# A merged group of score products, and a newly planned order of all instructions, in a causal attention that feeds a gated feed-forward block

## The chip, the cores and the metric

The kernel runs on one core of one Trainium2 chip. The metric is the device time of one execution in microseconds (us), lower is better. The core has a matrix engine (PE, with its weight loads as PEld), a vector engine (DVE), a scalar engine (ACT), a general engine (POOL) and a sequencer that issues every load and store here (SP). Each engine runs its own list of instructions in a fixed order; between engines there are only semaphores.

## The reference

```python
def _attn_ref(q, k, v):                      # 4 x 12 x 448 x 64, float32
    scores = (1 / sqrt(64)) * q @ k.T        # per batch and head, 448 x 448
    scores = where(above the diagonal, -1e9, scores)
    attn = exp(scores - max(scores))
    attn = attn / (sum(attn) + 1e-09)
    return attn @ v
x = attention output, heads side by side     # 1792 x 768
a, b = x @ w1, x @ w2                        # w1, w2: 768 x 1024
h = a * b @ w3                               # w3: 1024 x 1024
return h @ w_out                             # w_out: 1024 x 768
```

There is nothing between `w3` and `w_out`, so the kernel multiplies these two once (the "w34" product) and applies the result.

## The kernel before

**Stages.** (1) w34: blocks of w3 (index `m`, 128 rows, loaded in two halves) and of w_out (index `g`) are loaded and decoded (`decode`: two readings by ACT, a shift on DVE, an add on DVE or POOL). Each half block of w3 is turned on PE (L768, four transposes into the one bank of the pool `tr`), copied out (L774 on ACT or L775 on DVE), and multiplied with the blocks of w_out in float32 (L780). The first three blocks `m` are kept open together, in six banks. (2) Attention: 24 pairs of heads, six to a batch element. A pair loads q and k, turns them (L492 on PE for the first 12 pairs, by DMA for the rest), makes scores, the running maximum (L592, DVE) and exponential (L596, ACT), normalises and splits into two float16 halves (L621 to L628), turns these by DMA, and multiplies with v (L648, L653). (3) For each batch element the gates `x @ w1` and `x @ w2` (L904 to L906) and (4) the projection (L964 to L966), in float16 with three terms.

**Shapes of the array.** Most products use PE as one array of 128 x 128. The scores of two heads run side by side on two arrays of 64 rows (`mode="row"`), those of the last 64 queries on four arrays of 64 x 64 (`mode="quad"`), the products with v on two of 64 columns (`mode="col"`). The first 12 pairs make scores in float32, the others in float16.

**Score groups.** `scores` (L565) makes one entry of the plan per group of score units: for a pair the groups (2, 5), (1, 4), (6,) and (0, 3). Units 0 to 2 are the three chunks of 128 queries of one head (128, 256 and 384 keys wide), 3 to 5 those of the other, unit 6 the last 64 queries of both. Each unit has a bank of its own of the pool `sc`.

**Order.** Nothing is scheduled by the compiler. `Program.add` gathers entries with a due time, a cost for each engine that may run them, and their dependences. `Program.order` then plays the plan through on modelled engines: at each step the engine that is free first takes the ready entry with the earliest due time. That sets the order on every engine, which engine does a thing that several could do, and the banks. Due times come from `PLAN`, a table of numbers. `hold` adds a dependence that keeps the loads of an early pair behind the load of a chosen block of w_out. An SP entry waits in SP's list: a load or a DMA transpose that cannot go yet holds up all behind it.

Of the kernel before, what the change touches and what calls it, by code (L numbers as in the profile page):

```python
# [14 lines left out]
F16 = mybir.dt.float16  # L15
# [11 lines left out]
PLAN = dict(nc=10, wstep=3.6064, soft=-6.8718, w0=50.8305, w34=0.7706, ab=1.9504, out=0.6632, gap=-1.6322, lat=44.2335, begin=-91.0074, wlead=70.5419, urgent=-469.9817, flex=370.3401, sc=-41.0893, vo=-494.4237, av=-194.2706, x=-353.7633, qlead=-514.025, rlead=417.269, v0=250.3178, v1=137.6978, gram=2, nf=3, h0=0, hv=1, ns=7, wo0=372.2276, wo1=301.1492, wom=91.9573, w3a=767.9653, w3l=46.2422, wd=-104.1576, wh=-132.8946, wl=1.1959, fin=-10.7242, ev=483.517, po=[7.835, -22.3194, -46.2642, -45.7187, -46.1544, -168.5123, 44.732, 118.2718, -2.1469, -154.505, -36.8352, 4.8443, 45.9944, -62.3407, -59.3789, -141.4965, -13.9926, -146.366, -84.3586, -180.0751, 32.2385, 37.7583, 62.9194, 45.468], wo=[94.042, -8.263, -88.9315, -217.7217, 115.6771, 99.8526, 211.7957, -24.8481], w3=[-158.8005, -50.8167, -61.9442, -32.663, -51.9857, -143.9432, 16.037, 208.3012], tw=[-214.4914, 58.2404, 21.4694, -22.4979, -112.6908, -172.2348, -114.743, -134.9378, -53.1451, -19.9257, -4.9187, -20.2346, -61.9799, -199.5703, -107.2525, -134.2498], slack=0.1918, pflex=136.6935, fq=2, hlead=80.6809, stick=24.2514, wfrom=6)  # L27
# [10 lines left out]
WINDOW, PHASE = 3.413, 1.65  # L38

# [11 lines left out]
class Program:  # L51
# [3 lines left out]
    def __init__(self):  # L55
        self.ops, self.writer, self.readers, self.modes = [], {}, {}, {}
        self.port, self.lock = set(), set()
        self.banks, self.leased, self.first = {}, [], {}
# [5 lines left out]
    def add(self, due, how, reads=(), writes=(), stage=None, mode=None, port=False, lock=False):  # L64
# [18 lines left out]
        if mode:  # L83
            self.modes[i] = mode
        if port:
            self.port.add(i)
# [11 lines left out]
    def order(self):  # L98
# [8 lines left out]
        free = {e: 0.0 for e in (PE, ACT, DVE, POOL, SP)}  # L107
        soon = {e: [] for e in free}
        avail = {e: {} for e in free}
        ran = [None] * n  # L110
        dma_free, last_mode, lock_end, port_end = 0.0, None, 0.0, 0.0
# [28 lines left out]
        while len(result) < n:  # L140
# [41 lines left out]
            if e == SP:  # L182
                move, turn = cost
                dma_free = max(dma_free, t + (1.275 if turn else 1.1)) + move
                free[e] = max(t + 0.65, dma_free - 0.93) if turn else t + 0.475
                end = dma_free + 0.91
            else:
# [9 lines left out]
                if e == PE and cost:  # L197
                    mode = self.modes.get(i)
                    if mode != last_mode:
                        cost += SWITCH  # L200
                        last_mode = mode
                    end = matmul(t, cost)
# [40 lines left out]
def tile_causal_attention_moe(ctx: ExitStack, tc: tile.TileContext, q, k, v, w1, w2, w3, wo, out):  # L243
# [196 lines left out]
    def dma(dst, src, due, reads, writes, size, turn=False, rate=330e3):  # L440
        kw = {"transpose": True} if turn else {}
        prog.add(due, (SP, (size / (181e3 if turn else rate), turn),
# [15 lines left out]
    def take_v(b, half, due):  # L458
# [7 lines left out]
        for c in range(4):  # L466
            rows = min(P, S - c * P)
            dma(t[0:rows, c], v[b, heads, c * P : c * P + rows].rearrange("h p d -> p h d"), due - 6, (), [vk[c]],
                NP * rows * D * 4, rate=181e3)
# [11 lines left out]
    def turned_whole(p, b, hs, T, qk, qkk, qt, qtk):  # L481

        for i, src in ((1, k), (0, q)):
            dma(qk[0:QP, i], src[b, hs].rearrange("h (p r) d -> p r h d", r=4),
                T - PLAN["qlead"], (), [qkk + (i,)], 2 * S * D * 4, rate=181e3)
# [15 lines left out]
    def halved(p, b, hs, T, qk, qkk, qt, qtk):  # L501
# [4 lines left out]
        for i, src in ((1, k), (0, q)):  # L506
            raw_k = [qkk + (i, n) for n in range(3)]
            for h in range(2):
                dma(qk[:, i, 0:3, h], src[b, hs.start + h, 0 : 3 * P].rearrange("(c p) d -> p c d", p=P), T - PLAN["qlead"],
                    [], [raw_k[h]], 3 * P * D * 4, rate=181e3)  # L510
            dma(qk[0:D, i, 3], src[b, hs, 3 * P : S].rearrange("h p d -> p h d"), T - PLAN["qlead"],
                [], [raw_k[2]], 2 * D * D * 4, rate=181e3)
# [23 lines left out]
    def pair(p):  # L536
# [28 lines left out]
        def scores(us, due):  # L565
            i, c, w, lo = place(us[0])
            n = min(P, S - c * P)
            banks = [prog.lease("sc") for _ in us]
            m = mask_t if i == 2 else mask[:, (2 - c) * P :]

            def products(qs, ks, start, stop):
                for j in range(2):
                    rows = slice(j * D, (j + 1) * D)
                    ps = banks[j if i < 2 else 0][0]
                    nc.tensor.matmul(ps[rows if i == 2 else slice(0, P), :w], qs[rows, c * P : c * P + n], ks[rows, 0:w],  # L575
                                     start=start, stop=stop)

            def both():
                if not halves:
                    products(qt[:, 0], qt[:, 1], True, True)  # L580
                    return
                q16 = qt.rearrange("p i f -> p (i f)").bitcast(F16).rearrange("p (i t f) -> p i t f", i=2, t=2)
                for m_, (a, b_) in enumerate(((0, 0), (0, 1), (1, 0))):
                    products(q16[:, 0, a], q16[:, 1, b_], m_ == 0, m_ == 2)

            outs = [heads[place(u)[0]] for u in us]
            prog.add(due, (PE, (3 if halves else 4) * t_mm(w) + 0.02, both), [qtk + (1,), qtk + (0,)],
                     [key for _, key in banks] + [tk + (c,) for _, tk in outs] + ([tk for _, tk in outs] if p < 2 else []),
                     mode="quad" if i == 2 else "row")
            for u, (ps, key), (t32, tk) in zip(us, banks, outs):  # L590
                o = t32[:, lo : lo + w]
                prog.add(due + 0.4, (DVE, t_dve(w) + 0.07, lambda o=o, ps=ps, u=u: nc.vector.tensor_tensor_reduce(  # L592
                    out=o, in0=ps[:, :w], in1=m, scale=iv, scalar=-NEG,
# [471 lines left out]
```

## Time and profile before

| | |
|---|---|
| three runs | 554.55, 555.80, 556.99 us, median 555.8 |
| profiled execution | 555.84 us, its span 554.0 us |
| PE busy | 537.5 us (97%), 3872 instructions |
| DVE, ACT, POOL busy | 384.4, 323.9, 156.1 us (69%, 58%, 28%) |
| chain that ended last | PE 82%, DVE 9%, ACT 3%, DMA 3% |
| bytes moved by DMA | 84.60 MB |

The span runs from the first to the last instruction; 1.84 us of the execution's own time lie outside of it. The chain follows the work back from the last instruction, at each step to what released it or to the instruction before it on its engine. PE's records begin when an instruction starts to stream, and their ends overlap the next one's start; distances are therefore read from start to start.

### The profile page before, as it was taken

What the parts mean: (1) busy time and instruction counts of PE and PEld (TensorE: products, weight loads), DVE (VectorE), ACT (ScalarE), POOL (GpSimd) and SP (SyncE); (2) the same over time, 40 slices, a digit from 0 to 9 for tenths busy, and PEclk for the clock granted to TensorE, in tenths of its full rate; (3) what the DMA queues carried; (4) which work ended last, traced back from release to release, by engine and by line L of the source; (5) the groups of instructions that cost most, each with busy time, mean ns of one, the idle gap of its engine ahead of it and who ended that gap; (6) DMA issues with size and microseconds to landing.
All of it is one profiled execution on the core that took longest, in us unless ns stands there. A gap on an engine that the chain in (4) does not pass through costs nothing.

```text
span 554.0 us, 10756 instructions
## 1 busy us (share of the span) xinstructions
PE 537.5 (97%) x3872; PEld 300.5 (54%) x3872; DVE 384.4 (69%) x1057; ACT 323.9 (58%) x774; POOL 156.1 (28%) x118
## 2 busy tenths in 40 slices
PE   2999999999999999999999999999999999999996
PEld 1565565555554555555445555655555555555564
DVE  5536999998999899984998768398986760322100
ACT  6757888798698978654664646265762551111111
POOL 4000465554566424430334203231421110000000
PEclk9999999999999999999999999999999999999999
DMA  8998599989989648998777958979899235000011
GB/s 324 289 298 233 118 217 206 229 215 240 184 216 239 153 97 151 180 178 167 107 155 142 166 128 167 185 164 159 142 142 143 61 84 115 0 2 1 14 58 43
DMA packets 224950, 84.60 MB, mean 153 GB/s; under 512 B 205952, under 2 KB 221824, under 8 KB 224896
## 3 DMA queue, kind: packets, MB, share of 16 engines
q1 hardware_dynamic: 224896, 83.91, 72.1%
q8 instruction: 30, 0.49, 0.4%
q14 instruction: 24, 0.20, 0.1%
HBM read 43.78 MB, written 5.51 MB: 89 GB/s over the span
## 4 chain that ended last, share of the span: by engine, by line
PE 82%; DVE 9%; ACT 3%; DMA 3%; issue 1%; POOL 1%; POOLq 0%; ACTq 0%
PE sc L575 8%; PE mm L780 8%; PE mm L904 7%; PE mm L905 7%; PE mm L906 7%; PE mm L964 5%; PE mm L966 4%; PE mm L965 4%; PE tr L904 4%; PE av L653 4%; PE tr L905 4%; PE tr L906 4%; PE sc L780 2%; PE tr L964 2%; PE tr L966 2%; PE tr L965 2%
## 5 line engine op out<-in xcount | busy, mean ns | idle before, releaser
L906 PE MATMUL mm<-xt,w 128*128 128x448 f16 x258 | 90.9, 352 | 1.3 <-DVE w L727 1.3
L904 PE MATMUL mm<-xt,w 128*128 128x448 f16 x258 | 91.1, 353 | 0.0
L905 PE MATMUL mm<-xt,w 128*128 128x448 f16 x258 | 90.9, 352 | 0.0
L596 ACT ACTIVATE p<-p,mx 128x384 f32<-128x384 f32 (+2 forms) x144 | 71.5, 497 | 28.7 <-DVE mx L592 28.6
L780 PE MATMUL mm<-wof,w3t 128*128 128x384 f32 x192 | 71.4, 505 | 2.5 <-POOL wof L688 2.5
L628 DVE SCALAR_TENSOR_TENSOR ph<-p,rc,ph 128x384 f16<-128x384 f32 (+2 forms) x144 | 68.6, 528 | 1.4 <-ACT ph L623 0.9
L625 POOL TENSOR_SCALAR ph<-p,rc 128x128 f16<-128x128 f32 (+2 forms) x40 | 43.1, 1086 | 69.8 <-DVE rc L606 39.5
L575 PE MATMUL sc<-qkt 64*128 64x384 f16 (+7 forms) x480 | 58.9, 356 | 0.2 <-DMA qkt<-da 0.2
L906 PEld LDWEIGHTS <-w 128*128 128x128 f16 x384 | 37.5, 98 | 37.1 <-DVE w L727 2.2
L904 PEld LDWEIGHTS <-w 128*128 128x128 f16 x384 | 37.5, 98 | 36.0 <-issue 3.5
L905 PEld LDWEIGHTS <-w 128*128 128x128 f16 x384 | 37.5, 98 | 29.7 <-issue 0.2
L964 PE MATMUL mm<-w34h,arena 128*128 128x384 f16 x152 | 49.7, 327 | 0.0
L966 PE MATMUL mm<-w34h,arena 128*128 128x384 f16 x152 | 49.5, 326 | 0.0
L965 PE MATMUL mm<-w34l,arena 128*128 128x384 f16 x152 | 49.5, 326 | 0.0
L780 PEld LDWEIGHTS mm<-wof,w3t 128*128 128x128 f32 x192 | 34.2, 193 | 24.3 <-issue 4.1
L904 PE MATMUL tr<-xt,w 128*128 128x448 f16 x126 | 44.5, 353 | 0.0
L905 PE MATMUL tr<-xt,w 128*128 128x448 f16 x126 | 44.4, 352 | 0.0
L906 PE MATMUL tr<-xt,w 128*128 128x448 f16 x126 | 44.4, 352 | 0.0
L592 DVE CUSTOM_DVE_ANT_0 p<-sc,mask,qiv 128x384 f32<-128x384 f32 (+2 forms) x72 | 31.4, 478 | 18.0 <-PE sc L575 17.8
L930 ACT CAST arena<-g 128x448 f16<-128x448 f32 x22 | 12.4, 563 | 49.2 <-DVE g L925 49.2
L623 ACT ACTIVATE ph<-p,rc 128x384 f16<-128x384 f32 (+2 forms) x64 | 29.1, 504 | 9.5 <-issue 5.7
L685 DVE TENSOR_SCALAR da<-da 128x768 int32<-128x768 int32 (+1 forms) x38 | 24.2, 639 | 14.9 <-ACT da L681 14.7
(182 smaller groups left out, 1028.8 us busy)
## 6 DMA issues: line engine op xcount, KB each, us to landing
arena<-in_moe_w_dram SPq DMA_DIRECT2D x11, 768.0 KB, 5.7
vr<-in_v_dram SPq DMA_DIRECT2D x24, 192.0 KB, 3.9
out_dram<-osb SPq DMA_DIRECT2D x24, 192.0 KB, 2.2
arena<-in_moe_w_dram SPq DMA_DIRECT2D x8, 512.0 KB, 5.1
xt<-in_moe_w_dram SPq DMA_DIRECT2D x5, 768.0 KB, 8.0
qkr<-in_k_dram SPq DMA_DIRECT2D x12, 224.0 KB, 6.3
qkr<-in_q_dram SPq DMA_DIRECT2D x12, 224.0 KB, 6.9
arena<-in_moe_w_out_dram SPq DMA_DIRECT2D x3, 768.0 KB, 9.3
```

The lines of the kernel that those rows point to most:

```text
L575: nc.tensor.matmul(ps[rows if i == 2 else slice(0, P), :w], qs[rows, c * P : c * P + n], ks[rows, 0:w], start=start, stop=stop)
L592: prog.add(due + 0.4, (DVE, t_dve(w) + 0.07, lambda o=o, ps=ps, u=u: nc.vector.tensor_tensor_reduce(out=o, in0=ps[:, :w], in1=m, scale=iv, ...
L596: prog.add(due + 0.9, (ACT, t_act(w, pointers=1, acc=True), lambda o=o, u=u: nc.scalar.activation(out=o, in_=o, func=AF.Exp, scale=-1.0, b ...
L625: (POOL, 1.1 * (t_pool(w) + 0.35e-3 * w + 0.16), lambda src=src, r=r, h=h: nc.gpsimd.tensor_scalar(out=h, in0=src, scalar1=r, scalar2=None ...
L628: prog.add(due + 0.4, (DVE, t_dve(w) + 0.06, lambda src=src, r=r, h=h, l=l: nc.vector.scalar_tensor_tensor(out=l, in0=src, scalar=r, in1=h ...
L780: prog.add(due, (PE, 4 * t_mm(NH), lambda: nc.tensor.matmul(ps[:, :NH], w3t[slot(m)][:, g], wof[:, g, ns], start=g == 0, stop=g == KF - 1) ...
L904: nc.tensor.matmul(ps[:, :S], w[:, 0, d], xh, start=d == 0, stop=False)
L905: nc.tensor.matmul(ps[:, :S], w[:, 0, d], xl, start=False, stop=False)
L906: nc.tensor.matmul(ps[:, :S], w[:, 1, d], xh, start=False, stop=d == KD - 1)
L964: nc.tensor.matmul(t, gh[:, fc, cs], w34h[:, fc, ns], start=fc == 0, stop=False)
L965: nc.tensor.matmul(t, gh[:, fc, cs], w34l[:, fc, ns], start=False, stop=False)
L966: nc.tensor.matmul(t, gl[:, fc, cs], w34h[:, fc, ns], start=False, stop=fc == KF - 1)
```

## The change

The plan's table has new numbers throughout, and the planner's model of loads is new: a begin time for each engine, a rate and a count of descriptors for each kind of load, and a limit (`RING`) past which SP is held back. The model only decides the order. Two parts change what is built: `scores` now takes several groups for one entry, and the groups (1, 4) and (0, 3) form one, whose 128 columns stand behind the 256 in the same bank; and the group (6,) may also take the bank of the pool `tr`. With `h0=-1` and `hv=0` the first pair's loads, and the first half of v, are no longer held behind a block of w_out.

```diff
-PLAN = dict(nc=10, wstep=3.6064, ..., gram=2, nf=3, h0=0, hv=1, ns=7, ...)
+PLAN = dict(nc=10, wstep=10.6096, ..., gram=2, nf=3, h0=-1, hv=0, ns=7, ..., join=0)
...
+BEGIN = {PE: 1.3, ACT: 2.1, DVE: 0.85, POOL: 1.3, SP: 0.5}
+RING = 2150
...
             if e == SP:
-                move, turn = cost
-                dma_free = max(dma_free, t + (1.275 if turn else 1.1)) + move
-                free[e] = max(t + 0.65, dma_free - 0.93) if turn else t + 0.475
+                move, turn, count = cost
+                begun = max(dma_free, t + (1.07 if turn else 1.22))
+                dma_free = begun + move
                 end = dma_free + 0.91
+                if turn:
+                    free[e] = max(t + 0.65, dma_free - 0.6 - 0.5 * move)
+                else:
+                    free[e] = t + (0.6 if count > 800 else 0.43)
...
-    def dma(dst, src, due, reads, writes, size, turn=False, rate=330e3):
+    def dma(dst, src, due, reads, writes, size, turn=False, rate=430e3, count=128):
...
-        def scores(us, due):
-            i, c, w, lo = place(us[0])
-            banks = [prog.lease("sc") for _ in us]
+        def scores(groups, due):
+            blocks = []
+            for us in groups:
+                i, c, w, lo = place(us[0])
+                if c == 0:
+                    shared, at = blocks[-1][1], blocks[-1][2] + blocks[-1][4][2]
+                else:
+                    shared, at = [prog.lease("sc") if i < 2 else prog.lease("sc", "tr") for _ in us], 0
+                blocks.append((us, shared, at, mask_t if i == 2 else mask[:, (2 - c) * P :], (i, c, w, lo)))
...
-        for n, us in enumerate(((2, 5), (1, 4), (6,), (0, 3))):
-            scores(us, T + PLAN["sc"] + 0.6 * n)
+        for n, groups in enumerate(([[(2, 5)], [(1, 4), (0, 3)], [(6,)]], [[(2, 5), (6,)], [(1, 4), (0, 3)]])[PLAN["join"]]):
+            scores(groups, T + PLAN["sc"] + 0.6 * n)
```

Line numbers move: L575 becomes L602, L780 becomes L814, L768 becomes L802, L443 becomes L463, L681 and L683 become L714 and L716, L774 becomes L808.

**PE, scores of the first pair, before.** In the w34 stage; `qkt` holds turned q and k, rows of L575 are scores, L780 are w34 products, L768 and L492 turns.

```order
L575 MATMUL sc_69<-qkt_84 128x384
L575 MATMUL sc_66<-qkt_84 128x384
L407 LDWEIGHTS ones
L407 MATMUL sc_67<-w34m_126,ones 128x1
L780 MATMUL sc_68<-wof,w3t_124 128x384
L780 MATMUL mm_64<-wof,w3t_122 128x384 x2
L575 MATMUL sc_69<-qkt_84 128x256
L575 MATMUL sc_66<-qkt_84 128x256
L780 MATMUL mm_64<-wof,w3t_122 128x384
L768 MATMUL tr_70<-ident,arena 128x128 x4
L780 MATMUL mm_64<-wof,w3t_122 128x384
L575 MATMUL sc_67<-qkt_84 128x128
```

The same engine in the change, where the first pair's scores stand ahead of nearly all products of the stage:

```order
L602 MATMUL sc_66<-qkt_84 128x384
L602 MATMUL sc_67<-qkt_84 128x384
L602 MATMUL tr_70<-qkt_84 64x448 x2
L814 MATMUL mm_64<-wof,w3t_122 128x384
L814 MATMUL mm_65<-wof,w3t_122 128x384
L802 MATMUL tr_70<-ident,arena 128x128 x4
L602 MATMUL sc_66<-qkt_84 128x256
L602 MATMUL sc_67<-qkt_84 128x256
L602 MATMUL sc_66<-qkt_84 128x128
L602 MATMUL sc_67<-qkt_84 128x128
```

The 256- and 128-wide scores follow each other in one bank, and the tail (64x448) stands directly behind the 384-wide ones, in the bank `tr`.

**SP, the first loads, before.** `in_moe_w_dram` is w3 here, `in_moe_w_out_dram` w_out; the name on the left is the buffer that the raw words land in.

```order
L443 DMA arena<-in_moe_w_dram 128x1024 x2
L443 DMA xt_101<-in_moe_w_out_dram 128x1536
L443 DMA w34h<-in_moe_w_dram 128x1024
L443 DMA w34l<-in_moe_w_dram 128x1024
L443 DMA w34h<-in_moe_w_out_dram 128x1536
L443 DMA w34l<-in_moe_w_dram 128x1024
L443 DMA arena<-in_moe_w_dram 128x1024
L443 DMA arena<-in_moe_w_out_dram 128x1536
L443 DMA qkr_82<-in_k_dram 112x8x64
L443 DMA qkr_82<-in_q_dram 112x8x64
```

And in the change:

```order
L463 DMA w34l<-in_moe_w_dram 128x1024
L463 DMA arena<-in_moe_w_dram 128x1024 x2
L463 DMA xt_101<-in_moe_w_out_dram 128x1536
L463 DMA w34h<-in_moe_w_out_dram 128x1536
L463 DMA w34h<-in_moe_w_dram 128x1024
L463 DMA w34l<-in_moe_w_dram 128x1024
L463 DMA qkr_82<-in_k_dram 112x8x64
L463 DMA qkr_82<-in_q_dram 112x8x64
L463 DMA arena<-in_moe_w_dram 128x1024
L463 DMA arena<-in_moe_w_out_dram 128x1536
```

A half of the third w3 block (512 KB) now stands ahead of the two halves of the first; k and q of the first pair moved ahead of the third block's other half.

**ACT in the same stretch, before.** L681 and L683 are the two readings of a raw buffer, L774 copies turned w3 out of the bank `tr`.

```order
L683 ACTIVATE w34h<-w34h 128x768
L681 ACTIVATE da_107<-w34l 128x512
L774 COPY w3t_123<-tr_70 128x512
L683 ACTIVATE w34l<-w34l 128x512
L681 ACTIVATE da_108<-arena 128x512
L774 COPY w3t_123<-tr_70 128x512
```

In the change:

```order
L714 ACTIVATE p_88<-w34l 128x512
L716 ACTIVATE w34l<-w34l 128x512
L714 ACTIVATE da_108<-arena 128x512
L716 ACTIVATE arena<-arena 128x512
L808 COPY w3t_123<-tr_70 128x512
L714 ACTIVATE da_106<-arena 128x768
```

The first copy into `w3t_123` stands behind both readings of the third block's second half (`da_108`, `arena`); before it stood ahead of them.

## Rows read from the trace of the kernel before

**Rows 1.** PE's waits: line, for whom, us in total, times, longest.

```profile
PE tr L768 <- DVE arena L688: 6.7, 1, 6.7
...
PE mm L906 <- DVE w L727: 1.3, 2, 1.0
```

**Rows 2.** Stages: stretch, its length, then busy us of PE, PEld, DVE, ACT, POOL.

```profile
20.00:50.00 30.00, 29.94 (x116) 17.62 (x114) 11.84 (x20) 18.55 (x30) 1.28 (x1) 1.00 1.16 286
50.00:140.00 90.00, 90.00 (x569) 52.09 (x569) 84.01 (x231) 76.48 (x188) 45.47 (x29) 1.00 0.93 200
140.00:250.00 110.00, 108.53 (x849) 60.32 (x848) 104.77 (x285) 85.69 (x196) 52.50 (x33) 1.00 0.86 174
250.00:480.00 230.00, 229.78 (x1921) 126.13 (x1920) 163.85 (x488) 117.34 (x322) 51.23 (x42) 1.00 0.72 133
```

**Rows 3.** Timeline of PE, float32 part: start us, duration us, line, count.

```profile
52.91 0.70 PE L575 MATMUL sc<-qkt 64*128 64x256 f32 x4
53.54 0.91 PE L780 MATMUL mm<-wof,w3t 128*128 128x384 f32 x2
...
62.09 0.92 PE L575 MATMUL sc<-qkt 64*128 64x384 f32 x4
62.94 0.91 PE L780 MATMUL mm<-wof,w3t 128*128 128x384 f32 x2
63.69 0.60 PE L768 MATMUL tr<-ident,arena 128*128 128x128 f32 x4
...
72.92 1.35 PE L575 MATMUL sc<-qkt 64*128 64x256 f32 x8
74.20 0.91 PE L780 MATMUL mm<-wof,w3t 128*128 128x384 f32 x2
```

**Rows 4.** Timeline of PE, float16 products of the gates ahead of scores.

```profile
176.63 0.35 PE L905 MATMUL mm<-xt,w 128*128 128x448 f16 x1
176.82 0.35 PE L906 MATMUL mm<-xt,w 128*128 128x448 f16 x1
177.11 1.35 PE L575 MATMUL sc<-qkt 64*128 64x384 f32 x8
```

**Rows 5.** Chain that ended last, first 22 us: start us, duration us, what.

```profile
4.58 0.66 ACT da L681
...
6.67 1.10 PE tr L768 x4
...
12.01 2.93 PE mm L780 x4
...
15.83 0.59 ACT w3t L774
...
18.42 1.29 PE mm L780 x4
...
21.39 0.44 PE tr L768 x4
21.83 0.38 PE sc L492 x4
```

**Rows 6.** Landing times of the first two loads, issued at 0.73 and 1.19.

```profile
DMA to landing us min/median/max: 3.8/4.2/4.6
```

**Rows 7.** Loads issued from 7.7 to 9.2, and their times to landing.

```profile
L443 SPq DMA_DIRECT2D arena<-in_moe_w_out_dram x1: 328/328/328, 7.8 to 7.8; - x1
...
L443 SPq DMA_DIRECT2D qkr<-in_q_dram x1: 3105/3105/3105, 9.0 to 9.0; - x1
...
DMA to landing us min/median/max: 9.4/10.2/10.5
```

**Rows 8.** Groups by line and form on DVE and POOL: busy us, mean ns.

```profile
L621 DVE TENSOR_SCALAR ph<-p,rc 128x384 f16<-128x384 f32 x14 | 8.4, 608 | 0.1
...
L688 DVE CUSTOM_DVE_ANT_0 wof<-arena,da 128x1536 uint16<-128x1536 uint16 x3 | 2.9, 960 | 0.8 <-ACT arena L683 0.8
...
L688 POOL TENSOR_TENSOR wof<-da,xt 128x768 int32<-128x768 int32 x1 | 1.8, 1847 | 6.9 <-ACT xt L683 6.9
```

More of the change, by code (lines that the diff above doesn't have):

```diff
@@ L62, in lease, with add @@
         return l, l
[L64 removed]
+    def add(self, due, how, reads=(), writes=(), stage=None, mode=None, leave=None, port=False, lock=False):
         how = how if isinstance(how, list) else [how]
@@ L84, in add @@
             self.modes[i] = mode
+            self.leave[i] = leave or mode
         if port:
@@ L106, in order @@
         ready_at, done = [0.0] * n, [False] * n
-        free = {e: 0.0 for e in (PE, ACT, DVE, POOL, SP)}
+        free = dict(BEGIN)
         soon = {e: [] for e in free}
@@ L200, in order @@
                         cost += SWITCH
-                        last_mode = mode
+                    last_mode = self.leave.get(i)
                     end = matmul(t, cost)
@@ L574, in products @@
                     ps = banks[j if i < 2 else 0][0]
-                    nc.tensor.matmul(ps[rows if i == 2 else slice(0, P), :w], qs[rows, c * P : c * P + n], ks[rows, 0:w],
+                    nc.tensor.matmul(ps[rows if i == 2 else slice(0, P), at : at + w], qs[rows, c * P : c * P + n], ks[rows, 0:w],
                                      start=start, stop=stop)
             def both():
-                if not halves:
-                    products(qt[:, 0], qt[:, 1], True, True)
-                    return
@@ L582, in both @@
[L582 to L593, printed above, removed]
-                    op0=ALU.add, op1=ALU.min, accum_out=mx[:, u : u + 1])),
-                    [key, ivk, "mask_t" if i == 2 else "mask"], [mk + (u,), tk + (c,)] + ([tk] if p < 2 else []))
-                prog.add(due + 0.9, (ACT, t_act(w, pointers=1, acc=True), lambda o=o, u=u: nc.scalar.activation(
-                    out=o, in_=o, func=AF.Exp, scale=-1.0, bias=mx[:, u : u + 1], accum_out=sm[:, u : u + 1])),
-                    [mk + (u,)], [tk + (c,), smk + (u,)])
+                for block in blocks:
+                    if not halves:
+                        products(block, qt[:, 0], qt[:, 1], True, True)
+                        continue
+                    q16 = qt.rearrange("p i f -> p (i f)").bitcast(F16).rearrange("p (i t f) -> p i t f", i=2, t=2)
+                    for m_, (a, b_) in enumerate(((0, 0), (0, 1), (1, 0))):
+                        products(block, q16[:, 0, a], q16[:, 1, b_], m_ == 0, m_ == 2)
@@ new lines, in scores @@
+            keys = {id(l): l for b_ in blocks for _, l in b_[1]}
+            outs = [(heads[place(u)[0]][1], b_[4][1]) for b_ in blocks for u in b_[0]]
+            mode = ["quad" if b_[4][0] == 2 else "row" for b_ in blocks]
+            cost = sum((3 if halves else 4) * t_mm(b_[4][2]) + 0.02 for b_ in blocks) + SWITCH * (mode[0] != mode[-1])
+            prog.add(due, (PE, cost, both), [qtk + (1,), qtk + (0,)],
+                     list(keys.values()) + [tk + (c,) for tk, c in outs] + ([tk for tk, _ in outs] if p < 2 else []),
+                     mode=mode[0], leave=mode[-1])
@@ new lines, in scores @@
+            for us, banks, at, m, (i, c, w, lo) in blocks:
+                for u, (ps, key) in zip(us, banks):
+                    t32, tk = heads[place(u)[0]]
+                    o = t32[:, lo : lo + w]
+                    prog.add(due + 0.4, (DVE, t_dve(w) + 0.07, lambda o=o, ps=ps, u=u, at=at, w=w, m=m: nc.vector.tensor_tensor_reduce(
+                        out=o, in0=ps[:, at : at + w], in1=m, scale=iv, scalar=-NEG,
+                        op0=ALU.add, op1=ALU.min, accum_out=mx[:, u : u + 1])),
+                        [key, ivk, "mask_t" if i == 2 else "mask"], [mk + (u,), tk + (c,)] + ([tk] if p < 2 else []))
+                    prog.add(due + 0.9, (ACT, t_act(w, pointers=1, acc=True), lambda o=o, u=u: nc.scalar.activation(
+                        out=o, in_=o, func=AF.Exp, scale=-1.0, bias=mx[:, u : u + 1], accum_out=sm[:, u : u + 1])),
+                        [mk + (u,)], [tk + (c,), smk + (u,)])
```

38 lines of the change are left out of this document (26 added, 12 removed).

## The prediction

> **What bounds the kernel now.** I read the table of stages first, since one busy share over the whole program hides where an engine has room. PE is busy for 29.94 of 30 us from 20 to 50, for all of 50 to 140, for 108.53 of 110 from 140 to 250 and for 229.78 of 230 up to 480 [rows 2]. Behind 20 us it is idle for 0.06 + 1.47 + 0.22 = 1.75 us in all. The list of PE's waits says the same from the other side: one wait of 6.7 us at the start for the first decoded half block of w3, and later 1.3 us for the low halves of w1 and w2 (line 906), the rest being small or in the first 20 us [rows 1]. So the time is PE's work from about 20 us on, plus what PE has lost by then, plus a tail behind its last product that the change leaves as it is (the last projection, its eviction and stores stand in the same order). A gain can come from two places: less PE time for the same products, or an earlier start. A loss can come from a new wait. DVE is the engine that could cause one: it is busy for 84.01 of 90 us and 104.77 of 110 us in the two stages in which PE waits least [rows 2].
>
> **What a change of array shape costs.** A busy PE is not at its peak, and start distances show it. Among the gate products the step is 176.82 - 176.63 = 0.19 us, but the one ahead of scores takes 177.11 - 176.82 = 0.29: entering another shape costs 0.10 [rows 4]. In the float32 part more is lost. Four w34 instructions take 1.29 us when they follow their own kind, so two take 0.645 [rows 5]; the two that follow a score group take 63.69 - 62.94 = 0.75, again 0.10 more, this time behind the entry, at the second weight load [rows 3]. A 384-wide group that stands alone lasts 62.94 - 62.09 = 0.85, a 256-wide one 53.54 - 52.91 = 0.63, together 1.48; where the two stand side by side, in the row of eight, they last 74.20 - 72.92 = 1.28 [rows 3]. So joining two groups saves 0.20 inside, and with the entry and the slow second step of what comes between, a whole float32 visit that falls away is worth about 0.4.
>
> I then walked PE's list of instructions in both kernels and counted the places where the shape differs from that of the product before (the norms, which are the same in both, left out). Before: 168. In the change: 129. That is 39 fewer, at 0.10 each 3.9 us. Of entries into float32 scores of two heads there are 26 before and 16 in the change; w34 products are entered 9 and 11 times, the turns of float32 data 8 and 6 times. Net ten slow second steps fewer, at 0.10 each 1.0 us. The float16 entries show next to nothing at their second step, and I count nothing there. Sum: **-4.9 us**. The products themselves are as many as before, 3648 in both lists. This gain lies on the path as long as PE is the engine that never waits.
>
> The Trainium skill says that changing the tiling mode drains the engine (TensorEngine Tiling (Array Packing), Tiling Modes), and its page TensorE: Matmul & The Clock Gate (Single matmul latency) has a constant of 166 ns for one product at the full clock beside its columns. Taken as the price of a drain, an estimate from that page, 39 changes would be worth 6.5 us and the whole saving 7.5. The rows agree that a change of shape costs, but measure 0.10 at the entry, so the rows' figure is used.
>
> **The merged group by itself.** It also lets DVE read the 256-wide scores a little later, since both blocks now fill one bank: the 128-wide block takes 0.63 x 128/256, at most 0.3 us. Bounds: nothing, where DVE has other work, and 0.3 x 24 pairs = 7 us, if DVE stood idle for it each time and PE waited for DVE in turn. DVE is 93 to 95% busy in the tight stages [rows 2], so it has other work, and later PE doesn't wait for it: I take 0. Fewer banks are held by a pair, which can only help.
>
> **The start.** SP's first load is now a half of the third w3 block, ahead of the two halves of the first. The first two loads land at 0.73 + 3.8 = 4.5 and 1.19 + 4.6 = 5.8, so 512 KB take about 1.25 us in the queue [rows 6]. The decoding of the first half therefore starts at 5.8 and not at 4.58, and the first turn on PE, 6.67 - 4.58 = 2.1 us later, at 7.9 and not at 6.67 [rows 5]. The first product (12.01 before) waits for the first block of w_out. That too lands 1.25 us later, but its add now runs on DVE in 0.96 us and not on POOL in 1.85 [rows 8], so about 0.9 comes back: 12.3. The second block of w_out is now the fifth load and not the sixth, so its products follow at once. Against this stands ACT's order. The copy that frees the bank `tr` for the fourth group of turns is now behind both readings of the third block's other half. In the old queue the load behind that one landed at 7.8 + 9.4 = 17.2, and q, with k ahead of it, at 9.0 + 10.5 = 19.5: k and q take 2.3 us [rows 7]. The half block itself landed some 1.85 us ahead of 17.2 (768 KB at 512 KB in 1.23 us), at about 15.3; with k and q ahead of it, that becomes 17.6. Two readings of at most 0.66 each and the copy of 0.59 follow [rows 5]: 19.5. PE is through with what stands ahead by 12.3 + 2.9 (the first pair of products as slow as the old one) + 1.6 (the second pair, between 1.29 and 2.93) + 0.44 (third group of w3 turns) + 2 x 0.38 (turns of k and q) = 18.0 [rows 5], and waits some 1.4 us. Then I summed what PE has behind it at 22.2 us, the end of q's turns in the old chain (21.83 + 0.38): eight w34 products, five groups of w3 turns, and the turns of k and q [rows 5]. In the change the fourth group of turns starts at 19.5, four products of 2 x 1.29 follow it, and at 19.5 + 0.44 + 2.58 = 22.5 the same work is done but for the fifth group, 0.44 more [rows 5]: 22.96 against 22.2, and 0.1 for a change of shape that comes earlier. The start costs **+0.9 us**. Bounds from both sides: if the copy isn't late, the wait goes and the start is 0.4 us earlier; if every early step keeps the 1.25 us, and the bank `tr`, which now also holds tail scores, adds another wait of such a size, it is 2.5 later.
>
> **Behind the start.** Loads of w_out now come earlier in the queue, the first pair's scores stand ahead of most w34 products, and DVE, idle for 30 - 11.84 = 18.2 us between 20 and 50 [rows 2], gets attention work there. In return it gets more: by the lists five adds of 0.96 more (14, 9 before), seven 384-wide casts of 0.608 more (21 instead of 14) [rows 8], and seven copies out of PSUM of a like size, less four 128-wide casts and some single ones, net about 10 us in the first 250 us. The cover is those 18.2 us, so I cost it at 0; without cover it is a rival below. PE's later waits of 1.75 us [rows 2] I leave as they are: none of their places survives as it stands, so between 0 and 5 us is possible, with 1.75 as the nearest row.
>
> **Sum.** The profiled execution took 555.84 us (span 554.0 and 1.84 outside); the median of the three runs is 555.8, so nothing has to be corrected. 555.84 - 4.9 + 0.9 = **551.8 us**.
>
> **The rivals.** *The waits go as well* (12%): the plan keeps the saving, the copy isn't late and PE's later waits vanish: 555.84 - 4.9 - 0.4 - 1.75 = 548.8. For it speaks that every number of the plan was moved; against it that the start rests on the order alone, which shows the late copy.
>
> *The saving is given back in SP's list* (21%): loads of k and q that wait for a buffer which PE must first turn stand together in the change, and DMA transposes of the softmax behind them. A few waits of PE of 1 to 1.3 us, the size of that on line 906 [rows 1], three of them with the start's 0.9, and 555.84 - 4.9 + 0.9 + 3.5 = 555.3: no change. For it speaks that SP is the one list with no second engine; against it that the products with v come many products later than the transposes.
>
> *DVE becomes the bound* (20%): place, the stretch from 50 to 250; price, the 10 us of added work. There DVE has 6.0 + 5.2 = 11.2 us left of 200 [rows 2]. If the first pairs' attention doesn't get its data early enough to fill the idle 18.2 us, the added work comes to lie in this stretch and PE waits for scores, casts or low halves. It decides from the point at which PE's waits for DVE exceed the 4 us net saving. In full: 551.8 + 10 = 561.8; three quarters: 559.3, slower than before.
>
> **How the numbers follow.** What a measurement of this kernel can tell from no change is about 0.5%, 2.8 us: faster is below 553.0, slower above 558.6. The forecast has 47%, its own range is 550.3 to 554 (the start's bounds, and the waits from 0 to 2 us more); 36 of these are faster, 11 the same. Of the 12% of vanished waits all are faster. Of the 21% of the queue 17 are the same, 2 on either side. Of the 20% of DVE 16 are slower, 4 the same. Sum: faster 0.50, same 0.32, slower 0.18. The range for 8 in 10 is 548.5 to 560.0: it takes in the waits that go and most of the DVE case.
>
> **What the profile of the changed kernel would show.** For the saving: steps of two w34 instructions at 0.645 and of gate products at 0.19 nearly everywhere, and PE's busy time down by 3 to 5 us. For the start: the first turn at about 7.9, the first product at about 12.3, a wait of PE of about 1.4 us between 18 and 20 for the copy L808. For the cover: DVE busy for over 20 of the 30 us from 20 to 50, and PE's waits behind 20 us at about 2 us in sum. I am wrong on the saving if PE's waits are alike and its end isn't 4 us earlier; wrong on the cover if PE's list of waits has DVE or SP's transposes with over 4 us; and the order did not matter if PE's waits moved but their sum did not.

## The result, and the profile after

The changed kernel takes 561.38 us (median of 4 runs, 560.61 to 561.90) against 555.21 for the kernel before on the same chip: ratio **1.0105, 95% interval 1.0075 to 1.0134**, so 1.05% slower. The prediction was 551.8, faster. The profiled execution has a span of 559.1 us, 554.0 before.

PE's waits in the changed kernel (line, for whom, us in total, times, longest), to be held against [rows 1]:

```profile
PE tr L802 <- DVE arena L721: 7.9, 1, 7.9
PE av L681 <- DMA ptt<-pht: 2.8, 5, 1.3
PE sc L427 <- ACT da L414: 1.7, 3, 1.1
PE mm L814 <- DVE wof L721: 1.7, 1, 1.7
PE av L681 <- DVE ph L661: 1.4, 1, 1.4
PE tr L802 <- ACT w3t L808: 1.2, 1, 1.2
```

`av` is the product with v, `ptt` the last of the three turned softmax tiles of a pair. Before, no product with v waited for a DMA in this list; now there are five such waits. The one wait put down to DVE's `ph` (1.4 us, at 248.36) is a sixth of the same kind: that pair's `ptt` landed at 248.22. Together the six make 4.2 us. The stages, with the columns of [rows 2] (behind the five engines' busy times: granted clock, DMA share, GB/s):

```profile
20.00:50.00 30.00, 30.00 (x114) 16.85 (x114) 21.99 (x45) 24.25 (x45) 11.89 (x7) 1.00 1.14 291
50.00:140.00 90.00, 89.11 (x590) 53.51 (x589) 81.42 (x214) 70.73 (x169) 42.61 (x27) 1.00 1.00 213
140.00:250.00 110.00, 108.07 (x820) 60.80 (x818) 104.06 (x287) 83.68 (x194) 40.12 (x25) 1.00 0.71 163
250.00:480.00 230.00, 224.43 (x1903) 127.43 (x1902) 164.61 (x495) 117.54 (x316) 49.29 (x41) 1.00 0.71 134
```

DVE took its extra work where the prediction put it, between 20 and 50 us (21.99 us busy, 11.84 before). Of the 8.4 us that PE now lacks behind 20 us, 5.6 lie behind 250 us, where DVE has room.

I took every distance from one product's start to the next apart into the columns at the granted clock (1.00 in every slice, the 2.4 GHz level), the step at a change of shape, the recorded idle time, and the rest. In us:

| | before | changed | difference |
|---|---|---|---|
| first turn on PE | 6.67 | 7.92 | +1.25 |
| lost from there to 22 us | 7.37 | 7.42 | +0.05 |
| steps at changes of shape (168, 129) | 23.61 | 18.63 | **-4.98** |
| recorded idle time behind 22 us | 1.76 | 8.38 | **+6.62** |
| other slow steps (not taken apart further) | 11.94 | 14.08 | +2.14 |
| columns, and the tail | 502.68 | 502.68 | 0 |
| span | 554.03 | 559.11 | +5.08 |

So the saving came, to a tenth, and more than its size was lost in waits. One of them at close range. The changed kernel's SP list (queue, line, operation; start us, us), then PE, in the eleventh and twelfth pair:

```profile
239.93 5.04 SPq L463 DMA_TRANSPOSE pt<-ph  x2
245.07 1.27 SPq L463 DMA_TRANSPOSE ptt<-pht  x1
246.43 0.53 SPq L1016 DMA_DIRECT2D out_dram<-osb  x1
247.06 1.28 SPq L463 DMA_TRANSPOSE qkt<-da  x1
248.43 0.54 SPq L1016 DMA_DIRECT2D out_dram<-osb  x1
249.02 1.68 SPq L463 DMA_DIRECT2D qkr<-in_q_dram  x3
250.87 3.72 SPq L463 DMA_TRANSPOSE pt<-ph  x2
254.69 1.79 SPq L463 DMA_TRANSPOSE ptt<-pht  x1
```

```profile
257.55 0.35 PE L940 MATMUL mm<-xt,w 128*128 128x448 f16 x1
258.31 0.57 PE L681 MATMUL av<-ptt,v 128*64 128x64 f16 x24 [0.41 <-DMA ptt<-pht]
```

SP's list has no gap over 0.2 us here from one pair to the next. The transpose issued at 254.69 landed 3.6 us later, at 258.27, and PE stood for it. The same pair in the kernel before, SP and PE:

```profile
249.40 1.53 SPq L443 DMA_TRANSPOSE ptt<-pht  x1
...
256.09 0.57 PE L648 MATMUL av<-ptt,v 128*64 128x64 f16 x24
```

There it landed 3.4 us after its issue, at 252.8, and PE came 3.3 us later. I call this distance, from the landing of a pair's last transpose to PE's product with v, the margin. Over the pairs from the tenth on its median is 2.29 us before and 0.46 in the changed kernel; below 0.2 us are one pair before, where PE still had no idle time, and six now, where it stood for 0.2 to 1.4 us.

Where PE lost time the transfers were full. DMA share and GB/s are the last two columns; first the changed kernel, then the one before:

```profile
240.00:262.00 22.00, 20.15 (x194) 11.46 (x193) 18.14 (x56) 13.90 (x41) 4.40 (x6) 1.00 1.05 205
330.00:345.00 15.00, 14.94 (x141) 8.79 (x139) 11.76 (x40) 9.24 (x27) 4.27 (x4) 1.00 1.08 200
345.00:360.00 15.00, 13.81 (x162) 8.48 (x160) 14.27 (x38) 10.12 (x27) 7.38 (x6) 1.00 0.92 174
```

```profile
240.00:262.00 22.00, 22.00 (x221) 13.09 (x220) 12.53 (x39) 10.11 (x27) 3.59 (x3) 1.00 0.98 185
330.00:345.00 15.00, 15.00 (x111) 8.09 (x110) 13.55 (x52) 11.27 (x37) 4.05 (x4) 1.00 0.82 165
```

### The profile page after: what moved, and what is told of

Same layout as the page of the kernel before. It is cut to its first block, busy times and chain, and to the rows that moved or that the text cites. A ratio compares the mean times of both kernels' runs of the same rounds, so it can differ in the third digit from the quotient of the medians.

```text
span 559.1 us, 10750 instructions
## 1 busy us (share of the span) xinstructions
PE 534.7 (96%) x3872; PEld 305.0 (55%) x3872; DVE 391.8 (70%) x1076; ACT 320.6 (57%) x762; POOL 146.2 (26%) x111
## 5 line engine op out<-in xcount | busy, mean ns | idle before, releaser
L938 PE MATMUL mm<-xt,w 128*128 128x448 f16 x270 | 95.2, 353 | 0.0
L939 PE MATMUL mm<-xt,w 128*128 128x448 f16 x270 | 95.1, 352 | 0.0
L940 PE MATMUL mm<-xt,w 128*128 128x448 f16 x270 | 95.1, 352 | 0.0
L629 ACT ACTIVATE p<-p,mx 128x384 f32<-128x384 f32 (+1 forms) x144 | 71.3, 496 | 27.3 <-DVE mx L625 26.0
L814 PE MATMUL mm<-wof,w3t 128*128 128x384 f32 x192 | 70.1, 506 | 1.9 <-DVE wof L721 1.7
L658 POOL TENSOR_SCALAR ph<-p,rc 128x128 f16<-128x128 f32 (+2 forms) x40 | 36.4, 916 | 122.3 <-DVE rc L639 91.7
L661 DVE SCALAR_TENSOR_TENSOR ph<-p,rc,ph 128x384 f16<-128x384 f32 (+1 forms) x144 | 65.7, 518 | 0.5 <-ACT ph L656 0.3
L814 PEld LDWEIGHTS mm<-wof,w3t 128*128 128x128 f32 x192 | 35.2, 195 | 25.8 <-issue 3.0
L602 PE MATMUL sc<-qkt 64*128 64x128 f16 (+7 forms) x410 | 44.4, 343 | 1.6 <-DVE mx L625 0.7
L938 PE MATMUL tr<-xt,w 128*128 128x448 f16 x114 | 40.2, 353 | 0.0
L940 PE MATMUL tr<-xt,w 128*128 128x448 f16 x114 | 40.2, 352 | 0.0
L939 PE MATMUL tr<-xt,w 128*128 128x448 f16 x114 | 40.2, 352 | 0.0
L444 POOL TENSOR_SCALAR v<-vr,v_s 128x512 f16<-128x512 f32 x16 | 28.6, 1785 | 34.3 <-PE av L686 25.7
L656 ACT ACTIVATE ph<-p,rc 128x256 f16<-128x256 f32 (+2 forms) x59 | 27.4, 517 | 9.7 <-ACT p32t L629 3.7
```

Source lines behind the costliest of these rows:

```text
L602: nc.tensor.matmul(ps[rows if i == 2 else slice(0, P), at : at + w], qs[rows, c * P : c * P + n], ks[rows, 0:w], start=start, stop=stop)
L629: prog.add(due + 0.9, (ACT, t_act(w, pointers=1, acc=True), lambda o=o, u=u: nc.scalar.activation(out=o, in_=o, func=AF.Exp, scale=-1.0, b ...
L658: (POOL, 1.1 * (t_pool(w) + 0.35e-3 * w + 0.16), lambda src=src, r=r, h=h: nc.gpsimd.tensor_scalar(out=h, in0=src, scalar1=r, scalar2=None ...
L661: prog.add(due + 0.4, (DVE, t_dve(w) + 0.06, lambda src=src, r=r, h=h, l=l: nc.vector.scalar_tensor_tensor(out=l, in0=src, scalar=r, in1=h ...
L814: prog.add(due, (PE, 4 * t_mm(NH), lambda: nc.tensor.matmul(ps[:, :NH], w3t[slot(m)][:, g], wof[:, g, ns], start=g == 0, stop=g == KF - 1) ...
L938: nc.tensor.matmul(ps[:, :S], w[:, 0, d], xh, start=d == 0, stop=False)
```

## The experiments

The runs of the kernel before beside them had medians of 556.5 to 557.1 us, so ratios are compared, and the changed kernel's is 1.0105 throughout. The lists of the engines in these variants are the changed kernel's, entry for entry, but for what is named.

**1. SP's order alone.** Twelve moves in SP's list, made after the plan: a function puts an entry behind (L) or ahead of (E) the next few of its engine, together with all that depends on it.

```diff
+MOVES = [(1153, "L", 2), (2422, "L", 2), (2421, "L", 6), ...]
...
-        order = prog.order()
+        order = moved(prog, prog.order(), MOVES)
```

> The changed kernel with twelve entries of SP's list moved by a few places: loads of q, k and v and stores of the output that stood ahead of softmax transposes now stand behind them. The lists of PE, DVE, ACT and POOL are the same word for word. Theory A (behind 225 us SP's list is full: a load or store costs it about 0.6 us, so the transposes of the softmax leave late, and PE waits for them): PE's waits behind 22 us fall from 8.1 to 3.5 to 5 us, and the time from 561.4 to 556 to 558. Theory B (softmax itself is late, because DVE and ACT got 10 us more work): no change, 560.5 to 562.

Measured: 559.57 us, ratio 1.0046 (1.0023 to 1.0069). The four other lists are word for word the same, and over half of the loss is gone, 0.6% or 3.3 us. So SP's order alone is worth that much. Where it is gained the trace doesn't tell: it is of the fastest of ten executions (556.20 us), and of the 4.7 us that its PE is ahead of the changed kernel's at the end, it has 3.4 at 225 us, though all moved entries but one stand behind that. PE's idle time behind 225 us is 5.8 us against 7.0, so the 3.1 to 4.6 us fewer that theory A had expected did not show, and the median margin is 0.24 us, no larger than before the moves. Whether a softmax late on DVE and ACT (theory B) has a part in the loss is read from SP's waits, under run 3.

**2. Stores issued by ACT**, in both kernels.

```diff
-  lambda i=i, ns=ns, r=r, tok=tok, m=m: nc.sync.dma_start(
+  lambda i=i, ns=ns, r=r, tok=tok, m=m: nc.scalar.dma_start(
```

> The changed kernel with its 32 stores of the output issued by ACT and no longer by SP; nothing else is touched. Theory A (SP's list is full): SP gets rid of about eight stores at some 0.55 us between 225 and 262, and of as many in each later projection; PE's waits behind 22 us fall from 8.1 to 2 to 4 us, the time from 561.4 to 556 to 558. Theory B (DVE and ACT make the softmax late): ACT has 32 issues more, up to 16 us, so the waits stay or grow: 561 to 564.

> The control: the same edit in the kernel before, whose SP has idle time behind 225 us. Theory A: nothing to win, 554 to 557 (ACT's extra issues may cost up to 1.2 us). Theory B: 555 to 558. If it gains 4 us or more here too, the stores cost something that has nothing to do with the new order, and A is not shown by the other run.

Measured: 1.0112 (1.0078 to 1.0146) in the changed kernel, 0.9998 (0.9974 to 1.0022) in the one before. No gain, so theory A, that issues are what SP lacks time for, finds no support. By itself the run doesn't rule it out, since ACT issues 32 transfers more and theory B had expected 561 to 564 us (563.56 measured): at the 17th and the 24th pair SP stands for 3.3 and 4.0 us ahead of the transposes, for a softmax that isn't ready, and PE then for 1.4 and 0.3. But at the 10th to the 12th pair SP waits for nothing over 0.2 us and PE still stands for 2.6 us, 1.9 without the edit. In the profile SP has 32 entries fewer, but the waits for `ptt` are longer, and the transfers fuller:

```profile
PE av L681 <- DMA ptt<-pht: 5.3, 5, 1.6
```

```profile
240.00:262.00 22.00, 20.88 (x203) 12.09 (x200) 18.53 (x57) 14.61 (x43) 6.71 (x6) 1.00 1.13 204
```

Between 225 and 262 us a transpose took 4.93 us on average from issue to landing, 4.15 without the edit. What SP no longer issued went through the same transfer engines beside the transposes. The Trainium skill (DMA: Bandwidth & Descriptors, Issuing engines are not separate DMA queues) says just this: another issuing engine saves the time of the issue alone. The trace agrees so far as it shows the transposes landing later, 4.93 against 4.15, and not earlier. From here on theory A2: the transfers themselves, transposes above all, are what is full.

**3. Transposes of half the size**, in both kernels.

```diff
             o, ok = turned[i]
+            if b:
+                o, dst = o[:, 0:1], dst[:, 0:1]
```

> The changed kernel, in which the DMA transposes of the softmax move the high float16 half alone from the second batch element on (54 transposes of half the size; the low halves are left as they were turned for the first pairs, so this part of the products with v isn't computed). All lists keep their entries and order. Theory A2 (the transfers of the transposes, one behind the other in one queue that is full behind 225 us, set the end of PE's waits; how often SP issues is not the point): PE's waits behind 150 us, some 6 us, vanish, and the time falls by 5 to 6.5 us, ratio to the kernel before 0.999 to 1.002. Theory B (softmax late on DVE and ACT): less than 1.5 us.

> The control: the same edit in the kernel before. Theory A2: PE there hardly ever waits for a transpose, so the same relief is worth 0 to 1 us, ratio 0.998 to 1.000. If it gains as much as in the changed kernel, the transposes are a cost of both and don't explain the difference.

Measured: 552.89 us, ratio **0.9924** (0.9909 to 0.9939), in the changed kernel; 1.0005 (0.9986 to 1.0024) in the one before. It is the decisive pair: shorter transposes give the changed kernel 1.8%, more than the whole loss, and the kernel before nothing. Behind 225 us PE's idle time goes from 7.0 us (4.2 of them ahead of products with v, the rest ahead of scores and norms) to nothing. The waits that are left in the changed kernel lie in the first 22 us but for small ones, and in the stretches of above PE is busy throughout:

```profile
PE tr L804 <- DVE arena L723: 7.8, 1, 7.8
PE tr L804 <- DVE w3t L811: 1.8, 2, 1.6
PE mm L816 <- DVE wof L723: 1.5, 1, 1.5
PE sc L427 <- ACT w34h L414: 0.7, 1, 0.7
```

```profile
240.00:262.00 22.00, 22.00 (x221) 12.75 (x219) 17.65 (x57) 15.82 (x44) 5.39 (x5) 1.00 0.88 161
330.00:345.00 15.00, 15.00 (x184) 9.42 (x182) 14.85 (x46) 10.85 (x30) 7.76 (x6) 1.00 0.72 142
```

The median margin goes from 0.46 to 3.09 us (from 2.29 to 5.39 in the kernel before, where there was nothing to win). The expected 5 to 6.5 us were too few: the ratio says 10.

What the pair can't tell is which part of the way is too long. Half transposes move less, hold SP's list for less (147 us in sum over the program, 178 without the edit), and would also cover for a softmax that is late by as much as they are shorter. SP's waits in the changed kernel answer the last point. At five of the six pairs for which PE stands, SP waits for nothing over 0.2 us ahead of any of the three transposes: the softmax was ready before SP came to it. At the sixth, SP stands from 410.6 to 417.4 us for DVE's last half of the softmax, and PE for 1.31 us behind it:

```profile
409.95 0.61 SPq L463 DMA_DIRECT2D qkr<-in_q_dram  x1
417.45 3.72 SPq L463 DMA_TRANSPOSE pt<-ph  x2
421.26 1.82 SPq L463 DMA_TRANSPOSE ptt<-pht  x1
```

```profile
425.52 0.57 PE L681 MATMUL av<-ptt,v 128*64 128x64 f16 x24 [1.31 <-DMA ptt<-pht]
```

So theory B holds for this one wait; for the other 2.9 of the 4.2 us SP came to the transposes after the softmax was ready. In sum SP stood for the softmax less than before: from the tenth pair on 15.4 us ahead of its transposes, 28.8 in the kernel before. Between 225 and 262 us SP stood for 0.5 us in all, and for 5.9 in the kernel before.

**4. Stores left out.**

```diff
-  lambda i=i, ...: nc.sync.dma_start(
+  lambda i=i, ...: b == B - 1 and nc.sync.dma_start(
```

> The changed kernel without the stores of the first three batch elements' output (22 of 32 stores, 3.9 MB; these rows aren't written); nothing else is moved. The stores issued by ACT took the issue off SP and left the transfer, and won nothing. Theory A2 (it is the transfers in the queue that hold the transposes back): now it falls by 3 to 7 us. If neither the issue nor the transfer of the stores matters, it stays within 1.5 us, and A2 has to be cut down to the transposes themselves.

Measured: 555.42 us, ratio 0.9977 (0.9956 to 0.9998), 7 us less than the changed kernel. With run 2: taking the issue off SP wins nothing (with ACT's share in that), taking the transfer away too wins more than the loss. PE's idle time behind 22 us is 2.9 us; the 1.31 us behind the late softmax are still among it. The same edit was not made in the kernel before, so how much of the 7 us stores cost there too stays open.

**5. The merged groups apart again.** `late` is the block (0, 3) of a merged group; it goes behind the next product of the whole array.

```diff
+            if late and e == PE and i not in prog.modes and prog.ops[i][1][0][1]:
+                order.append(late)
...
+            if i in twos:
+                order[-1] = (t, i, e, lambda f=twos[i]: f(0), end)
+                late = (t, i, e, lambda f=twos[i]: f(1), end)
```

> The changed kernel with the 128-wide block of each of its 24 merged groups put apart again, behind the next product of the whole array; all other entries keep their places. Changes of array shape go from 129 to 173. By the prediction's prices (0.10 a change, another 0.10 at the second float32 step, twice for each of 12 pairs) PE's work grows by 4.3 to 6.5 us. Theory A (the loss lies in SP's list, PE is not the only bound): waits shrink by 2 to 3 us as PE comes later, so 563.5 to 565.5. Theory C (the merged group is itself the cause of the loss): the time falls below 560.

Measured: 565.7 us, ratio 1.0150 (1.0124 to 1.0175). The steps at changes of shape grow by 6.1 us, 0.14 for each of the 44, and the time by 2.5 (by the ratios; the two profiled spans are 5.2 apart). PE's idle time behind 22 us shrank by 1.2 us, to 7.2, less than the 2 to 3 expected; the rest of the difference isn't accounted for. Theory C, which had the time fall below 560, fell; the merge is worth its price on PE, and the changed kernel loses elsewhere.

**6. The first load.** The half of the third w3 block goes behind the two halves of the first, and so does its reading by ACT.

```diff
+MOVES = [(48, "L", 2), (50, "L", 4)]
...
+        order = moved(prog, prog.order(), MOVES)
```

> The changed kernel with the half block of the third w3 block, its first load, moved behind the two halves of the first block, as in the kernel before; the reading of it by ACT moves behind theirs. First turn on PE at 6.7 and not at 7.9. If the start's loss hangs on that load, the time falls by 0.9 to 1.3 us; by the chain it is the first block of w_out that starts the products (12.8), and it still lands behind the same three loads, so I expect 0 to 0.5 us, ratio 1.009 to 1.011.

Measured: 562.56 us, 1.0101 (1.0057 to 1.0145). The first turn is at 6.71, and little is won: PE then waits 3.0 us for the first block of w_out instead of 1.7, and at 22 us it is 0.36 us ahead of the changed kernel. The median can't show so little; in the profiled execution PE also ran at 1.2 instead of 2.4 GHz for 3.4 us from 249.7 on, behind a wait of 2.1 us (granted clock 0.83 from 245 to 255 us).

**7. Better orders.** Moves in all lists, of the changed kernel (228, then 509) and of the one before (113). They were chosen by playing the lists through: each entry starts when its engine is free and what it needs is there, and takes as long as in the traces.

```diff
+        order = moved(prog, prog.order(), MOVES)
```

> The changed kernel with 228 single moves of entries by a few places in the lists of all engines, found by playing the lists through with the durations of the changed kernel's trace and with transposes that hold SP 0.3 us longer than the planner has it, and keeping a move where the end came earlier also with slower transposes, a 2% slower DVE and later semaphores. Played so, the kernel before comes out at 549.5 us for PE's end (549.8 in its trace), the changed one at 554.4 (554.9), this at 542.9, its changes of shape 118. Theory A2: PE's waits behind 22 us fall below 1.5 us, and the time to 547 to 552, ratio 0.983 to 0.993, better than both. If the merged group or the new numbers carry a loss that isn't a wait, it stays above 556.

> The changed kernel with the 228 moves of the run before (moved_after) and 281 more, chosen with the durations averaged over four traces of the changed kernel's variants and with loads of weights 12% and other loads 5% slower, since the last version still waited 6.9 us behind 22 us where 0.5 were played. Played through with these harder transfers, PE's end is 555 us for the changed kernel, 547 for moved_after and 543.4 to 550 for this. Theory A2 (transposes and loads in one full queue): waits behind 22 us fall below 4 us and the ratio to the kernel before is 0.980 to 0.993, lower than moved_after's 0.9972. If the moves have nothing more to win, it comes out within 0.3% of moved_after.

> The same kind of moves (113, chosen in the same way) in the kernel before, without the merged group and the new numbers; its changes of shape go from 168 to 152. If the merged groups are worth what the prediction says (some 5 us of PE's work), this can't reach the moved version of the changed kernel: played through, PE's end goes from 549.5 to 547.3, ratio 0.992 to 0.999. If it comes out as low as moved2_after, the merge isn't needed for that gain.

Measured: 0.9972 (0.9952 to 0.9993), 0.9977 (0.9957 to 0.9997) and 0.9970 (0.9949 to 0.9991). All three are a little faster than the kernel before. The two moved versions of the changed kernel are slower than worked out (0.983 to 0.993, 0.980 to 0.993), the moved kernel before came out as expected (0.992 to 0.999). In the profile of the first, PE spends 6.5 us less than the kernel before on changes of shape and waits 6.9 us behind 22 us:

```profile
PE av L716 <- DMA ptt<-pht: 1.3, 3, 0.8
PE sc L637 <- DMA qkt<-da: 1.2, 1, 1.2
...
PE av L716 <- DVE ph L696: 1.1, 1, 1.1
```

Transposes again, and the softmax ahead of them, among other small waits. That playing the lists through doesn't see how a moved transfer slows those it then meets is my reading of the miss; no run shows it by itself. So the changed kernel's order can be mended by 1.3%, but what its merged groups save is still paid back in waits, and the same sort of moves brings the kernel before as far.

**8. More transfers in the kernel before.**

```diff
+  [nc.sync.dma_start(out=..., in_=...) for _ in range(2 if b < B - 1 else 1)]
```

> The mirror of the run without stores, in the kernel before: each of the 22 stores of the first three batch elements is issued twice, so 3.9 MB more go through SP's queue, in the places where the stores stood; all lists keep their order. In the kernel before the last transpose lands 1.7 to 4 us ahead of most products with v, and its DMA share between 240 and 262 us is 0.98. Theory A2 says how near that is to the edge: the extra transfers (22 times some 0.5 to 1 us) must show as waits of PE for transposes, 2 to 12 us, ratio 1.004 to 1.022. If the kernel before has an ample reserve, it stays within 1.5 us; then a full queue alone does not make the loss, and the order behind the transposes has to be looked at again.

Measured: 587.58 us, ratio 1.0536 (1.0506 to 1.0567), far above what I expected. It doesn't tell what it was made for: the second store of a pair waited in SP's list until the first had landed, which is another thing than more bytes (the DMA share from 240 to 262 us was 0.89):

```profile
SPq L982 <- DMA out_dram<-osb: 39.8, 22, 3.8
```

What it shows is that 39.8 us in which SP's list stands cost 30 us here, and not by waits alone. Behind 22 us PE's idle time grew by 21.6 us; and during three waits of 5.4 to 7.4 us the granted clock fell to the lower level (1.2 GHz), where it stayed for 15 us of PE's work behind them: an estimate of 7.5 us. The first of the three lies in this stretch (granted clock 0.85):

```profile
262.00:285.00 23.00, 17.32 (x108) 8.62 (x107) 13.60 (x44) 11.11 (x29) 4.30 (x4) 0.85 0.66 121
```

How many more bytes the kernel before could bear stays open.

## Why the prediction was wrong

**Changes of shape: right.** -4.9 was predicted and -4.98 measured, and 44 changes put back cost 0.14 each, near the 0.10 and the second float32 step of [rows 3, 4]. The estimate of 7.5 us from the 166 ns of the Trainium skill (TensorE: Matmul & The Clock Gate, Single matmul latency) was too high by half.

**The start: right in its places, a little too small.** First turn at 7.92 (7.9 predicted), first product at 12.84 (12.3), a wait of 1.2 us for the copy L808 at 19.85 (1.4). PE's timeline:

```profile
7.92 1.09 PE L802 MATMUL tr<-ident,arena 128*128 128x128 f32 x4 [7.92 <-DVE arena L721]
...
12.84 4.61 PE L814 MATMUL mm<-wof,w3t 128*128 128x384 f32 x8 [1.72 <-DVE wof L721]
...
19.85 0.66 PE L802 MATMUL tr<-ident,arena 128*128 128x128 f32 x4 [1.19 <-ACT w3t L808]
```

The sum is +1.3 instead of +0.9. Run 6 adds that the first load, on which my chain began, hardly sets it (0.36 us); the block of w_out does.

**DVE's cover: right in its place, not shown to be free.** DVE was busy for 22.0 us from 20 to 50. By the prediction's own sign, over 4 us of waits for DVE or for SP's transposes, the cover was wrong: the six waits of products with v alone make 4.2 us. For five of them SP came to the transposes after the softmax was ready, for one DVE's softmax was late (1.31 us). The rival that DVE becomes the bound from 50 to 250 us did not come about, and that its price was near the result is chance. One reading in the first paragraph was wrong, though no term rests on it: from 140 to 250 us PE waited 1.47 us, the most and not the least of the stages behind 20 us [rows 2].

**Behind the start: the step that failed.** "PE's later waits of 1.75 us [rows 2] I leave as they are" stood in the sum; they became 8.38, and slow steps of another 2.1 came with them. What the runs put in its place: of the 8.38 us, 7.0 lie behind 225 us, and all of these go when the transposes are halved (run 3). I had even written "between 0 and 5 us", which was too narrow. The rival of SP's list named the place (transposes of the softmax behind loads of k and q), but at three waits of about 1 us, 3.5 us, and with a sentence that made it unlikely: the products with v "come many products later than the transposes". That was read from the lists. Counted in time it was 2.3 us before and 0.46 in the change, and a list shows no time. What I did not look at was the DMA column of the stage view, which stood there with 1.16, 0.93 and 0.86 up to 250 us [rows 2]: with transfers so full, a transpose's landing was a thing to be followed pair by pair. Behind 250 us, where most of the waits came, its mean of 0.72 would not have shown it; the 0.98 from 240 to 262 us does.

**What the planner did.** I treated its new model of loads as a matter of order alone. It also decides how close the order dares to come to a landing. By its own played times the plan was to take 545.3 us, the old one 548.4; the chip took 559.1 and 554.0. The old plan put the product with v a median of 0.7 us behind the planned landing and got 2.0 on the chip; the new one put 1.5 us and got 0.9. From issue to landing a 448 KB transpose was planned well in both: a median of 4.7 us where the chip took 4.4, and 4.8 where it took 4.6. What slipped is the time at which SP comes to the issue. From the tenth pair on the last transpose was issued a median of 2.9 us later than in the old plan, and PE's product started 4.9 us later than there; in the change these are 11.4 and 10.3 us, so the landing slipped more than PE did. (SP and PE wait for each other, so this doesn't say which slipped first.) The old plan had a reserve in SP's list: a 448 KB transpose held it for 2.9 us, on the chip for 2.25 on average. The new one has a median of 2.2 us, the chip an average of 2.2, and nothing is left over for an issue of few descriptors, which holds the planned SP for 0.43 us, while three loads of q held it 1.68 us in the rows above, 0.56 each. That these numbers made the plan too tight is my reading; no run changed them alone, because each such number reorders everything.

## What to carry to other kernels

Costs in a planner that are too high can be a reserve, and making them exact can spend it (a reading here, not a test); so when a model of transfers is replaced, compare the margins, from each landing to the instruction that needs it, before and after. When a change shortens an engine that never waits, look at what runs full beside it (here DMA share 0.98 in the stretch that then failed): the saving ends where that becomes the bound. To tell whether issues or transfers are what is short, move the issue to another engine and, in another run, take the transfer away. And look at what the issuing list waited for at each late landing, since a shorter transfer also hides data that come late.

## What the runs showed of the hardware

A softmax transpose of 448 KB landed 4.5 us (median, from the second batch element on) after its issue and one of 224 KB 3.1 us: 1.4 us for 224 KB, an estimate of some 160 GB/s. The Trainium skill (Advanced Engine Details and Errata, X-Bar Transpose (TRN2)) expects 350 to 400 GB/s; these runs, with loads beside the transposes and earlier transposes ahead of them in the queue, show less than half of that.

```profile
pt<-ph SPq DMA_TRANSPOSE x48, 4.6
ptt<-pht SPq DMA_TRANSPOSE x24, 3.6
```

```profile
pt<-ph SPq DMA_TRANSPOSE x48, 3.2
ptt<-pht SPq DMA_TRANSPOSE x24, 2.5
```

The first two rows are the changed kernel's, the others those of run 3 (buffers, operation, count, median us to landing); in run 3, 12 of the 48 and 6 of the 24 are whole. And in the changed kernel a transpose held SP's list for 1.2 to 4.2 us (the very first, behind the weights' loads, for 7.3), a load for 0.57 in the median. Two softmax transposes in a row took up 5.04 us of SP's list at 239.93, above, and it had waited for nothing ahead of either: transposes that follow one another wait inside the list, where no wait is shown.
